# Block maxima of an attention layer: the float16 split moved to GpSimd, the turn moved behind the next burst of scores, the copy moved to ScalarE

## The chip, the cores and the metric

The kernel runs on one core of one Trainium2 chip. The core has five engines that run their own instruction streams and meet at semaphores: TensorE (PE in the profile, with its weight loads listed apart as PEld), VectorE (DVE), ScalarE (ACT), GpSimd (POOL) and SyncE (SP), which here only issues DMAs. Each engine works through its instructions in program order, so an instruction that waits holds up everything behind it on its engine. The metric is the device time of one execution in microseconds, the median of several runs.

## What is computed

```python
x = A_x                                            # 1 x 2048 x 512
xn = _layernorm(x, axis=-1)
# attention, 32 heads of 16
qkv = (xn @ wqkv).reshape(B, S, 3, H, Dh).transpose(2, 0, 3, 1, 4)
scores = einsum("bhqd,bhkd->bhqk", q, k) * Dh ** -0.5
o = einsum("bhqk,bhkd->bhqd", softmax(scores), v)
attention = o.transpose(0, 2, 1, 3).reshape(B, S, D) @ wo
# dense part, 512 -> 1792 -> 512
dense = gelu(xn @ w1 + b1) @ w2 + b2
return x + attention + dense
```

The softmax needs, for each query and head, the largest score over all 2048 keys before the exponentials are taken. How this maximum reaches the exponentials is what the change is about.

## The kernel before

**Blocks and units.** A block `t` is four heads (a group `g`) by 512 queries; there are 8 x 4 = 32 blocks. The attention loop is `unit` (line 766), called once for each of 32 x 16 = 512 units `u`. A unit does one sixteenth of two blocks at once. For block `u // 16` it forms four pieces of scores (`s_half`, one for each head: 128 queries by 512 keys into a PSUM bank of the "S" rotation) and VectorE takes the largest along the keys (`s_max`, line 366) into `mt`. For the block of unit `e = u - 19` (`LEAD` is 19) it forms the transposed scores again (`e_half`, 128 keys by 512 queries into a bank of the "T" rotation), ScalarE takes the exponential (line 414), and TensorE multiplies the exponentials of a unit or two earlier with the values (`v_half`, into `pV`). So a block's maxima are complete three units before its first exponential.

**Two halves of a unit.** TensorE's part of a unit is two halves. Each half begins with a burst of four score pieces (E, S, S, E) and goes on with `v_half` on 64 rows of the array beside the dense work (`dense`: projections, the hidden layer, the second product, the output projection) on the other 64 rows. How many dense products a half takes is the pace: `FAST` four, `SLOW` three, `MEAN` three and four by turns. All products of the loop have line 169 (`tiled`); tiles tell them apart: `pS<-kst,qst`, `pT<-qst,kst`, `pV<-pe,vv`, `pD`.

**The maxima.** The maximum is not subtracted by an instruction of its own: it is written, as two float16 numbers (a high part and the rest), into two spare rows of the stacked queries `qst`, and a constant in the same rows of `kst` makes the product subtract it. The way there, for each block: when the last piece of scores is reduced, `s_end` (line 375) takes the largest of the four partial maxima, negated, into `mneg` (line 382, VectorE). In the next unit, after its first half, `store` (lines 385 to 399) runs: TensorE turns `mneg` with an identity (line 390, float32) into a PSUM bank, VectorE splits the result into the two float16 parts (lines 393 and 394), SyncE stores them to DRAM in two DMAs (line 397) and, once these have landed, loads them into the rows of `qst` in four DMAs, one for each head (`m_rows`, line 348). `e_half` of the block's first unit waits for these loads.

**Which bank.** The turn takes a bank of the S or of the T rotation, three banks each: S where the dense group has just begun (`fresh`, line 387), T otherwise. A bank can be written when its last reader is done: VectorE for S, ScalarE for T.

**GpSimd's work** (splitting weights, GELU, scaling the attention output) is queued as steps; `run_steps` (line 315) lets out up to `POOL_NS` (2500 ns by the kernel's own estimates) for each unit.

**The first block** goes through a planner (`Plan`, line 215) that orders the prologue of the program by estimated times; lines 1130 to 1152 give it the same chain with costs.

Of the kernel before, what the change touches and what calls it, by code (L numbers as in the profile page):

```python
# [18 lines left out]
P = 128  # L19
# [15 lines left out]
POOL_NS = 2500  # L35
TAIL = 5
# [18 lines left out]
def layer_kernel(ctx: ExitStack, tc: tile.TileContext, x, wqkv, wo, w1, b1, w2, b2, out):  # L55
# [19 lines left out]
    m_d = dram.tile([NG * NQB, 16, 2, P], F16, name="m_d")  # L75
# [21 lines left out]
    mnegs = [const.tile([P, 32], F32, name=f"mneg{i}") for i in range(2)]  # L97
    for m in mnegs:
        nc.gpsimd.memset(m, 0.0)
# [244 lines left out]
    def m_rows(t, h):  # L344
# [3 lines left out]
        nc.sync.dma_start(dst, m_d[t, 4 * h:4 * h + 4].rearrange("t r q -> r t q"))  # L348
# [11 lines left out]
    def s_max(u, n, s):  # L360
# [5 lines left out]
        nc.vector.reduce_max(mt_of[t][:, n, qt, kb:kb + 1], s, axis=AX.X)  # L366
# [8 lines left out]
    def s_end(u):  # L375
# [4 lines left out]
        g, qb = divmod(t, NQB)  # L380
        mneg = mnegs[t % 2]
        nc.vector.tensor_reduce(mneg[:, :16], mt_of[t].rearrange("p h t k -> p (h t) k"), axis=AX.X, op=ALU.max, negate=True)
        given("dve", 220)

        def store():

            fresh = cur[0] is not None and 0 < sum(cur[0].at) <= 4
            pt = banks("S" if fresh else "T")
            for a in range(2):
                nc.tensor.matmul(pt[32 * a:32 * a + 32, :64], mneg[64 * a:64 * a + 64, :],  # L390
                                 ident[64 * a:64 * a + 64, 64 * a:64 * a + 64], start=True, stop=True)
            mhl = work.tile([64, 2, 64], F16, name="mhl", bufs=2)
            nc.vector.tensor_scalar_mul(mhl[:, 0], pt[:64, :64], 1.0 / MROW)
            nc.vector.scalar_tensor_tensor(mhl[:, 1], pt[:64, :64], 1.0 / MROW, mhl[:, 0], op0=ALU.mult, op1=ALU.subtract)
            given("dve", 300)
            for a in range(2):
                nc.sync.dma_start(m_d[t, :, :, 64 * a:64 * a + 64], mhl[32 * a:32 * a + 16])
            for h in range(4):
                m_rows(t, h)
# [366 lines left out]
    def unit(gen):  # L766
# [7 lines left out]
        for a in range(2):  # L774
            for kind, b in ((1, 1), (0, 0), (0, 1), (1, 0)) if a == 0 else ((1, 2), (0, 3), (0, 2), (1, 3)):
# [4 lines left out]
                elif not kind and u > NU:  # L780
                    spare(gen, b % 2)
            if e >= 0:
# [23 lines left out]
            if a == 0 and u % 16 == 0 and u // 16 - 1 in stores:  # L806
# [711 lines left out]
```

## Time and profile before

| | |
|---|---|
| median of 3 runs | 1454.23 us (1451.61 to 1455.41) |
| the profiled execution | 1450.86 us, of it the profile's span 1449.1 us |
| mean granted TensorE clock | 0.996 |
| 31 final reductions, line 382 | 220 ns each |
| 31 pairs of split instructions, lines 393 and 394 | 207 and 217 ns each |
| 62 stores, line 397 | 591 ns median issue time each |
| 128 loads, line 348 | 258 ns median issue time each |

The profile lists for each engine how long it was busy, groups of like instructions with their mean duration, who waited for whom, and the instructions in order of time. A row of such a timeline has the start (us from the span's start), the length, the engine, the line, the operation with its output and inputs, a count where like instructions were merged, and in brackets the idle time ahead with what ended it.

### The profile page before, as it was taken

The page shows a single profiled execution, that of the slowest core. Times are in us where ns is not written, and L with a number is a line of the kernel's source. Part 1 is how long each engine was busy: PE and PEld are TensorE (multiplying, and loading weights), DVE is VectorE, ACT ScalarE, POOL GpSimd, SP SyncE. Part 2 cuts the span into 40 slices and gives each one's busy share as a digit, 9 for nine tenths or more (in the row PEclk, how much of TensorE's full clock was granted, in tenths as well). Part 3 has the DMA queues.
Part 4 walks back from the last instruction along what each step waited for, and adds up shares of the span by engine and source line. Part 5 has one row for each costly group of instructions (what it writes and reads, how often), then busy time and mean ns, then how long its engine had stood idle before and what let it go on. Part 6 is the DMA issues. An engine that isn't in the chain of part 4 may idle for free.

```text
span 1449.1 us, 88687 instructions
## 1 busy us (share of the span) xinstructions
PE 1432.0 (99%) x40184; PEld 964.6 (67%) x40184; DVE 1353.8 (93%) x2304; ACT 1255.9 (87%) x2367; POOL 663.8 (46%) x673
## 2 busy tenths in 40 slices
PE   8999999999999999999999999999999999999998
PEld 4447767776666767667677766676766767666565
DVE  7989999999999999999999999999999999999933
ACT  5868888888999888899988899998889999888885
POOL 3201857664878401388831138882115787121100
PEclk9999999999999999999999999999999999999999
DMA  7731565455224210221112111121112110111423
GB/s 218 226 122 40 163 202 182 150 181 153 86 64 131 67 34 27 62 70 42 45 44 89 30 37 46 55 74 45 44 39 85 48 38 23 56 55 47 137 65 119
DMA packets 112627, 124.86 MB, mean 86 GB/s; under 512 B 22908, under 2 KB 84220, under 8 KB 112248
## 3 DMA queue, kind: packets, MB, share of 16 engines
q1 hardware_dynamic: 112248, 119.18, 26.8%
q8 instruction: 314, 5.14, 1.5%
q14 instruction: 65, 0.53, 0.1%
HBM read 81.66 MB, written 37.34 MB: 82 GB/s over the span
## 4 chain that ended last, share of the span: by engine, by line
PE 87%; DVE 8%; DMA 2%; ACT 1%; issue 1%; SPq 0%; DVEq 0%; ACTq 0%
PE pD L169 26%; PE pV L169 25%; PE pT L169 17%; PE pS L169 16%; DVE mt L366 7%; PE pT L1015 2%; DMA wq<-in_A_wqkv_dram 1%; PE pD L1015 1%; DMA m_d<-mhl 0%; ACT xs L968 0%; DVE xt L998 0%; ACT pe L414 0%; DMA qst<-m_d 0%; DVE ac L1393 0%; ACT wqk_h L904 0%
## 5 line engine op out<-in xcount | busy, mean ns | idle before, releaser
L366 DVE TENSOR_REDUCE mt<-pS 128x1 f32<-128x512 f32 x2029 | 1277.4, 682 | 34.8 <-PE pS L169 7.8
L414 ACT ACTIVATE pe<-pT 128x512 f32<-128x512 f32 x2048 | 1106.9, 599 | 150.2 <-PE pT L169 65.0
L169 PE MATMUL pV<-pe,vv 64*32 64x512 f32 x8192 | 1087.8, 591 | 0.3 <-issue 0.2
L169 PE MATMUL pT<-qst,kst 64*32 64x512 f16 x8192 | 710.4, 378 | 1.9 <-issue 1.2
L169 PE MATMUL pS<-kst,qst 62*32 62x512 f16 x8116 | 627.0, 378 | 2.6 <-DVE mt L366 2.0
L169 PEld LDWEIGHTS <-qst 62*32 62x32 f16 x8192 | 309.3, 90 | 196.7 <-issue 50.9
L169 PE MATMUL pD<-xb,wc 64*32 64x512 f16 x5376 | 363.9, 375 | 0.0
L169 PE MATMUL pD<-w_s,g 64*32 64x512 f16 x5376 | 361.8, 375 | 0.0
L169 PEld LDWEIGHTS <-kst 64*32 64x32 f16 x8192 | 280.5, 91 | 96.0 <-issue 24.2
L169 PEld LDWEIGHTS pV<-pe,vv 64*32 64x32 f32 x8192 | 245.3, 105 | 13.6 <-PE pV L169 4.2
L169 PEld LDWEIGHTS <-wc 64*32 64x32 f16 x5376 | 160.7, 91 | 44.5 <-issue 0.4
L169 PEld LDWEIGHTS <-g 64*32 64x32 f16 x5376 | 163.5, 91 | 39.2 <-issue 0.5
L169 PE MATMUL pD<-xt,wqk_h 64*32 64x512 f16 x2400 | 159.3, 376 | 0.7 <-issue 0.7
L1360 POOL TENSOR_TENSOR xa<-xa,yt 128x512 f32<-128x512 f32 x16 | 20.5, 1281 | 222.8 <-ACT yt L1358 222.8
L471 POOL TENSOR_TENSOR osb<-osb,rb 128x512 f32<-128x512 f32 x31 | 39.9, 1286 | 159.2 <-DMA rb<-den_d 132.8
L1312 POOL TENSOR_TENSOR t<-hh 128x512 f32<-128x512 f32 x56 | 58.2, 1040 | 77.0 <-ACT hh L1335 75.9
L169 PEld LDWEIGHTS <-wqk_h 64*32 64x32 f16 x2400 | 74.0, 92 | 19.9 <-issue 2.0
L1314 POOL TENSOR_TENSOR t<-t,hh 128x512 f32<-128x512 f32 x56 | 71.8, 1282 | 4.7
L1307 POOL TENSOR_TENSOR t<-t,hh 128x512 f32<-128x512 f32 x56 | 71.7, 1280 | 4.7
L1309 POOL TENSOR_TENSOR g<-t,g 128x512 f16<-128x512 f32 x56 | 65.2, 1164 | 4.7
L1306 POOL TENSOR_SCALAR t<-t,gs 128x512 f32<-128x512 f32 x56 | 38.8, 694 | 54.8 <-ACT t L1301 54.8
L169 PE MATMUL pD<-wo_s,oc 64*32 64x512 f16 x816 | 54.7, 376 | 0.0
(165 smaller groups left out, 895.1 us busy)
## 6 DMA issues: line engine op xcount, KB each, us to landing
wc<-w_d SPq DMA_DIRECT2D x56, 256.0 KB
qk_d<-stg SPq DMA_DIRECT2D x32, 256.0 KB
rb<-den_d SPq DMA_DIRECT2D x124, 64.0 KB
wch<-in_B_w_dram SPq DMA_DIRECT2D x14, 512.0 KB
wch<-in_B_w_dram SPq DMA_DIRECT2D x28, 256.0 KB
w_d<-wsp SPq DMA_DIRECT2D x28, 256.0 KB
kst<-qk_d SPq DMA_DIRECT2D x64, 96.0 KB
qst<-qk_d SPq DMA_DIRECT2D x64, 96.0 KB
```

The source lines that it names most:

```text
L169: p = nc.tensor.matmul(*args, **kw)
L366: nc.vector.reduce_max(mt_of[t][:, n, qt, kb:kb + 1], s, axis=AX.X)
L414: nc.scalar.activation(pe, st, AF.Exp, scale=scale_of[g // 2])
L471: pooled((1280, lambda: nc.gpsimd.tensor_tensor(osb, osb, rb, op=ALU.mult)), (620, lambda: nc.gpsimd.tensor_scalar(ot[:, 0], osb, 1.0, 0.0 ...
L1015: nc.tensor.matmul(tl[key], lhs, rhs, start=c + n == 0, stop=(c, n) == (NC - 1, 2))
L1306: pooled((690, lambda: nc.gpsimd.tensor_scalar(t1, t1, 1.0, gs[:, 1:2], op0=ALU.add, op1=ALU.mult)), (1280, lambda: nc.gpsimd.tensor_tenso ...
L1307: (1280, lambda: nc.gpsimd.tensor_tensor(t1, t1, hh, op=ALU.mult)),
L1309: (1160, lambda: nc.gpsimd.tensor_tensor(g[:, 1, f, :], t1, g[:, 0, f, :], op=ALU.subtract)),
L1312: pooled((1040, lambda: nc.gpsimd.tensor_tensor(t1, hh, hh, op=ALU.mult)), (620, lambda: nc.gpsimd.tensor_scalar(t1, t1, 1.0, 1.0 / GELU_A ...
L1314: (1280, lambda: nc.gpsimd.tensor_tensor(t1, t1, hh, op=ALU.mult)),
L1360: add = lambda: nc.gpsimd.tensor_tensor(xa, xa, yt, op=ALU.add)
```

## The change

The maxima take another way from `mt` to `qst`. VectorE still takes the largest of the partial maxima (now `mx`, not negated). GpSimd then scales it and makes the two float16 parts, in three instructions on 128 partitions by 16 numbers, put on its queue at the end of the block's last unit, without regard to the allowance of `run_steps`. TensorE turns the float16 parts with a negated float16 identity (`nident`); this now stands behind the burst of the second half of the next unit, ahead of that half's `v_half` and dense work. ScalarE copies the turned parts out of PSUM (64 x 64). One DMA stores them, and two load them (one for each half of the partitions). The allowance of GpSimd's steps becomes 800 ns in the unit before a block's last, and 3100 ns in the three units from the block's last on. The first block's chain in the planner is changed alike. The order of the heads in `mt` is swapped so that a half of the partitions holds its two heads side by side.

```diff
+POOL_AT = {15: 800, 0: 3100, 1: 3100, 2: 3100}
...
-    m_d = dram.tile([NG * NQB, 16, 2, P], F16, name="m_d")
+    m_d = dram.tile([NG * NQB, 2, 2, 2, 8, P // 2], F16, name="m_d")
...
+    nident = const.tile([P, P // 2], F16, name="nident")
+    for a in range(2):
+        nc.gpsimd.tensor_scalar(nident[64 * a:64 * a + 64], ident[64 * a:64 * a + 64, 64 * a:64 * a + 64], -1.0, 0.0,
+                                op0=ALU.mult, op1=ALU.add)
...
     def run_steps(all_of_them=False):
-        room[0] = min(room[0], 0) + POOL_NS
+        room[0] = min(room[0], 0) + (POOL_AT.get(pos[0] % 16, POOL_NS) if pos[0] < NU else POOL_NS)
...
+    def m_store(t, turned):
+        nc.sync.dma_start(m_d[t].rearrange("s a j r q -> (s a j r) q"), turned)
+
+    def m_rows(t, a):
         g, qb = divmod(t, NQB)
-        p, a = divmod(h, 2)
-        dst = qst[g % 2][qb][64 * a + 62:64 * a + 64, p].rearrange("r (t q) -> r t q", q=P)
-        nc.sync.dma_start(dst, m_d[t, 4 * h:4 * h + 4].rearrange("t r q -> r t q"))
+        dst = qst[g % 2][qb][64 * a + 62:64 * a + 64].rearrange("j p (t s q) -> j (p t) s q", s=2, q=P // 2)
+        nc.sync.dma_start(dst, m_d[t, :, a].rearrange("s j r q -> j r s q"))
+
+    def m_parts(t):
+        mx = work.tile([P, 2, 8], F32, name="mx", bufs=1)
+        parts = work.tile([P, 2, 2, 8], F16, name="mparts", bufs=2)
+        return (lambda: nc.vector.tensor_reduce(mx.rearrange("p a r -> p (a r)"), mt_of[t].rearrange("p h t k -> p (h t) k"),
+                                                axis=AX.X, op=ALU.max),
+                lambda: nc.gpsimd.tensor_scalar(mx, mx, 1.0 / MROW, 0.0, op0=ALU.mult, op1=ALU.add),
+                lambda: nc.gpsimd.tensor_scalar(parts[:, :, 0], mx, 1.0, 0.0, op0=ALU.mult, op1=ALU.add),
+                lambda: nc.gpsimd.tensor_tensor(parts[:, :, 1], mx, parts[:, :, 0], op=ALU.subtract)), parts
+
+    def m_turn(pt, parts):
+        for s in range(2):
+            nc.tensor.matmul(pt[32 * s:32 * s + 32, :64], parts[64 * s:64 * s + 64].rearrange("p a j r -> p (a j r)"),
+                             nident[64 * s:64 * s + 64], start=True, stop=True)
+
+    def m_copy(pt):
+        turned = work.tile([64, 64], F16, name="mturned", bufs=2)
+        nc.scalar.activation(turned, pt[:64, :64], AF.Copy)
+        return turned
...
     def s_end(u):
...
-        mneg = mnegs[t % 2]
-        nc.vector.tensor_reduce(mneg[:, :16], mt_of[t].rearrange("p h t k -> p (h t) k"), axis=AX.X, op=ALU.max, negate=True)
+        steps, parts = m_parts(t)
+        for step in steps:
+            step()
...
             pt = banks("S" if fresh else "T")
+            m_turn(pt, parts)
+            m_store(t, m_copy(pt))
             for a in range(2):
-                nc.tensor.matmul(pt[32 * a:32 * a + 32, :64], mneg[64 * a:64 * a + 64, :],
-                                 ident[64 * a:64 * a + 64, 64 * a:64 * a + 64], start=True, stop=True)
-            mhl = work.tile([64, 2, 64], F16, name="mhl", bufs=2)
-            nc.vector.tensor_scalar_mul(mhl[:, 0], pt[:64, :64], 1.0 / MROW)
-            nc.vector.scalar_tensor_tensor(mhl[:, 1], pt[:64, :64], 1.0 / MROW, mhl[:, 0], op0=ALU.mult, op1=ALU.subtract)
-            given("dve", 300)
-            for a in range(2):
-                nc.sync.dma_start(m_d[t, :, :, 64 * a:64 * a + 64], mhl[32 * a:32 * a + 16])
-            for h in range(4):
-                m_rows(t, h)
+                m_rows(t, a)
...
     def unit(gen):
...
+            if a == 1 and u % 16 == 0 and u // 16 - 1 in stores:
+                stores.pop(u // 16 - 1)()
             if e >= 0:
                 one_more()
                 enter()
...
             if a == 0:
                 run_lane()
-            if a == 0 and u % 16 == 0 and u // 16 - 1 in stores:
-                stores.pop(u // 16 - 1)()
```

**TensorE, block 11, first unit of the next block.** Before, the turn (`ident,mneg`) stands between the first half's dense products (`pD`) and the second half's burst (`pT` first; `kst_3_82` and `qst_2_89` are two of the stacked tiles).

```order
L169 LDWEIGHTS g
L169 MATMUL pD<-w_s,g 32x512
L390 MATMUL pT<-ident,mneg_101 32x64 x2
L169 LDWEIGHTS kst_3_82
L169 MATMUL pT<-qst_2_89,kst_3_82 32x512
```

With the change the last rows of that burst come first, then the turn, then the second half's products with the values.

```order
L171 LDWEIGHTS kst_3_82
L171 MATMUL pT<-qst_2_89,kst_3_82 32x512
L366 LDWEIGHTS mparts
L366 MATMUL pT<-nident,mparts 32x64
L366 LDWEIGHTS mparts
L366 MATMUL pT<-nident,mparts 32x64
L171 MATMUL pV<-pe,vv 32x512 x4
L171 LDWEIGHTS g
L171 MATMUL pD<-w_s,g 32x512
```

The turn moved behind one burst of 16 products; nothing else moved between the two places. Apart from these turns TensorE's rows after the prologue are the same in both.

**VectorE, the same block.** Before, two instructions of the split stand behind the first two reductions of the next block's scores.

```order
L458 RECIPROCAL dn<-dn 64x32
L366 TENSOR_REDUCE mt<-pS 128x1 x20
L382 TENSOR_REDUCE mneg_101<-mt 128x16
L366 TENSOR_REDUCE mt<-pS 128x1 x2
L393 TENSOR_SCALAR mhl<-pT 64x64
L394 SCALAR_TENSOR_TENSOR mhl<-pT,mhl 64x64
L366 TENSOR_REDUCE mt<-pS 128x1 x42
```

With the change all 44 reductions up to the next reciprocal follow the final one without a break.

```order
L475 RECIPROCAL dn<-dn 64x32
L390 TENSOR_REDUCE mt<-pS 128x1 x20
L358 TENSOR_REDUCE mx<-mt 128x16
L390 TENSOR_REDUCE mt<-pS 128x1 x44
L475 RECIPROCAL dn<-dn 64x32
```

VectorE lost the two split instructions and kept the rest in place.

**GpSimd at the end of block 8.** These are the rows of the changed kernel: the last step of one piece of GELU, the three new instructions, and the next piece of GELU (`t` and `hh` are its work tiles, `osb` is attention output to be scaled).

```order
L1318 TENSOR_TENSOR g<-t_12839,g 128x512
L360 TENSOR_SCALAR mx<-mx 128x16
L361 TENSOR_SCALAR mparts<-mx 128x2x8
L362 TENSOR_TENSOR mparts<-mx,mparts 128x2x8
L1321 TENSOR_TENSOR t_13494<-hh 128x512
L1322 TENSOR_SCALAR t_13494<-t_13494 128x512
L1323 TENSOR_TENSOR t_13494<-t_13494,hh 128x512
L488 TENSOR_TENSOR osb<-osb,rb 128x512
```

Before, the rows of GELU followed each other directly; the three new ones now stand between them, and the first of the three waits for VectorE's final reduction.

More of the change, by code (lines that the diff above doesn't have):

```diff
@@ L95, in layer_kernel @@
     sexp = const.tile([P, 4], F32, name="sexp")
-    mnegs = [const.tile([P, 32], F32, name=f"mneg{i}") for i in range(2)]
-    for m in mnegs:
-        nc.gpsimd.memset(m, 0.0)
+    nident = const.tile([P, P // 2], F16, name="nident")
+    for a in range(2):
+        nc.gpsimd.tensor_scalar(nident[64 * a:64 * a + 64], ident[64 * a:64 * a + 64, 64 * a:64 * a + 64], -1.0, 0.0,
+                                op0=ALU.mult, op1=ALU.add)
     free_banks = {"S": [0, 1, 2], "T": [3, 4, 5], "D": [6], "V": [7]}
```

31 lines of the change are left out of this document (11 added, 20 removed).

## The prediction

> **What bounds the kernel now.** I read the page first (busy shares), then the waits, then the timelines of VectorE, TensorE and ScalarE around the ends of three blocks.
>
> ```profile
> PE 1432.0 (99%) x40184; PEld 964.6 (67%) x40184; DVE 1353.8 (93%) x2304; ACT 1255.9 (87%) x2367; POOL 663.8 (46%) x673
> ```
>
> TensorE is never long without work, VectorE is close behind. So a gain must come from stretches in which TensorE runs below its pace, which a busy share hides. What the waits name at the maxima is small:
>
> ```profile
> PE pS L169 <- DVE mt L366: 2.0, 5, 1.2
> PEld L169 <- DMA qst<-m_d: 2.8, 5, 0.9
> ```
>
> (columns: us in total, times, longest). The loads of the maxima cost 2.8 us in five places. Pace says more. In block 11, in the stage where the dense work alternates between three and four products, the starts of the value products tell the halves apart:
>
> ```profile
> 548.50 0.66 PE L169 MATMUL pV<-pe,vv 64*32 64x512 f32 x4
> 550.89 0.65 PE L169 MATMUL pV<-pe,vv 64*32 64x512 f32 x4
> 552.34 0.60 PE L169 MATMUL pV<-pe,vv 64*32 64x512 f32 x3
> 553.89 0.61 PE L169 MATMUL pV<-pe,vv 64*32 64x512 f32 x4
> 556.28 0.61 PE L169 MATMUL pV<-pe,vv 64*32 64x512 f32 x4
> 558.89 0.68 PE L169 MATMUL pV<-pe,vv 64*32 64x512 f32 x4
> ```
>
> Units of 2.39 us (548.50 to 550.89, 553.89 to 556.28) alternate with one of 2.61 (556.28 to 558.89). The unit with the turn takes 3.00 (550.89 to 553.89) where 2.62 is due: 0.38 too much. VectorE and TensorE at that place:
>
> ```profile
> 551.24 0.22 DVE L382 TENSOR_REDUCE mneg<-mt 128x16 f32<-128x64 f32 x1
> 551.37 1.28 DVE L366 TENSOR_REDUCE mt<-pS 128x1 f32<-128x512 f32 x2
> 552.57 0.21 DVE L393 TENSOR_SCALAR mhl<-pT 64x64 f16<-64x64 f32 x1
> 552.95 13.23 DVE L366 TENSOR_REDUCE mt<-pS 128x1 f32<-128x512 f32 x21
> 553.67 0.40 PE L169 MATMUL pS<-kst,qst 62*32 62x512 f16 x4
> ```
>
> I call the start of L382 T. The split holds VectorE from 552.57 to 552.95, 0.38 us. The reduction that starts at 552.95 (0.68 us by the mean below) ends at 553.63, and the score piece at 553.67 starts 0.04 later: it waited for that bank.
>
> ```profile
> L366 DVE TENSOR_REDUCE mt<-pS 128x1 f32<-128x512 f32 x2029 | 1277.4, 682 | 34.8 <-PE pS L169 7.8 <-PE pT L169 6.5 <-PE pV L169 2.3
> ```
>
> Where the dense work takes four products in every half, TensorE is slower than VectorE and the loss is smaller. Block 22, by the starts of every second pair of exponentials (so unit by unit), and two more rows of that place:
>
> ```profile
> 1003.57 1.08 ACT L414 ACTIVATE pe<-pT 128x512 f32<-128x512 f32 x2 [0.27 <-PE pT L169]
> 1006.18 1.08 ACT L414 ACTIVATE pe<-pT 128x512 f32<-128x512 f32 x2 [0.27 <-PE pT L169]
> 1008.97 1.09 ACT L414 ACTIVATE pe<-pT 128x512 f32<-128x512 f32 x2 [0.37 <-PE pT L169]
> 1011.59 1.09 ACT L414 ACTIVATE pe<-pT 128x512 f32<-128x512 f32 x2 [0.27 <-PE pT L169]
> 1006.22 0.22 DVE L382 TENSOR_REDUCE mneg<-mt 128x16 f32<-128x64 f32 x1
> 1007.43 0.66 PE L169 MATMUL pV<-pe,vv 64*32 64x512 f32 x4
> ```
>
> 2.61, 2.79, 2.62: 0.18 too much. The third kind is the turn in a bank of S, seven of the 31 blocks behind the first:
>
> ```profile
> L393 DVE TENSOR_SCALAR mhl<-pS 64x64 f16<-64x64 f32 x7 | 1.5, 207 | 0.1
> 922.16 0.61 PE L169 MATMUL pV<-pe,vv 64*32 64x512 f32 x4
> 922.64 1.28 DVE L366 TENSOR_REDUCE mt<-pS 128x1 f32<-128x512 f32 x2
> 923.98 0.40 PE L169 MATMUL pS<-kst,qst 62*32 62x512 f16 x4 [0.20 <-DVE mt L366]
> 924.19 0.61 PE L169 MATMUL pV<-pe,vv 64*32 64x512 f32 x4
> ```
>
> The turn takes one of three banks, so the last score piece of the burst needs the bank of the reductions that end at 923.92 (922.64 + 1.28). This half takes 2.03 us (922.16 to 924.19) against some 1.31 (half of 2.62): 0.7 too much. With 14, 10 and 7 blocks of the three kinds (the 14 and 10 are my sorting of the other 24 by their dense work) the block ends cost 14 x 0.38 + 10 x 0.18 + 7 x 0.7 = 12 us. That bounds the gain from above, with 2.8 for the loads.
>
> **The change part by part. VectorE** loses 0.38 us at each block end, and its reductions come that much earlier. **GpSimd** gets three instructions of 128x16, which the trace doesn't have; the nearest rows are
>
> ```profile
> L472 POOL TENSOR_SCALAR ot<-osb 128x512 f16<-128x512 f32 x31 | 19.1, 618 | 2.7
> L1218 POOL TENSOR_SCALAR wsp<-wch 128x1024 f16<-128x1024 f32 x14 | 14.6, 1045 | 1.1
> L473 POOL TENSOR_TENSOR ot<-osb,ot 128x512 f16<-128x512 f32 x31 | 36.1, 1164 | 2.6
> L1219 POOL TENSOR_TENSOR wsp<-wch,wsp 128x1024 f16<-128x1024 f32 x14 | 30.0, 2141 | 1.2
> ```
>
> One source: 1045 - 618 = 427 ns for 512 numbers more, so 618 - 427 = 191 ns remain for none, and 16 numbers make 204. Two sources: 977 for 512, 187 for none, 218 for 16. Between dependent steps the 31 rows of L473 show 2.6 us of idle time, 0.08 each; I take 0.08 for every hand-over, between engines too (the piece above needed 0.04). From T: 0.22 + 0.08 + 0.20 + 0.08 + 0.20 + 0.08 + 0.22 + 0.08 = 1.16 us until TensorE may load the parts. My bounds are 0.7 (half of 204 for each, and 0.04 a hand-over) and 1.8 (twice 204 each): estimates from these rows in both directions.
>
> The Trainium skill, "GPSIMD Engine Reference", section 4.1, says that elementwise work belongs on VectorE, with GpSimd about twice as slow for two inputs. The trace agrees in kind for wide tiles (L473's 1164 ns against 684 for VectorE's two-source row below); for 16 numbers no row shows it. By that rule the parts would come later than 1.16, which is the second rival.
>
> ```profile
> L998 DVE TENSOR_TENSOR xt<-pT,xt 128x512 f16<-128x512 f32 x6 | 3.9, 684 | 0.0
> ```
>
> **The turn.** When does TensorE come to it? In block 11 the value products that follow it start at T + 1.10 (552.34), in block 22 at T + 1.21 (1007.43). The float32 turn ahead of the burst leaves; in block 22, 0.18 covers it and the reductions, so I give it 0.1. The natural place is T + 1.0 and T + 1.1, the parts are ready at 1.16, and with 0.05 for two small float16 products the values start at T + 1.21: 0.11 later than now in the first kind, unchanged in the second. All that stands behind the turn on TensorE (values, dense work, the next burst) waits with it.
>
> In the first kind the next half then no longer waits for VectorE: the bank that was free at 553.63 is free at 553.25. The values due at T + 1.21 = 552.45 plus 1.31 are at 553.76, against 553.89: 0.13 gained. Second kind: only the rest behind the turn can go, which I put at half of 0.18, 0.09. Third kind: the turn, now behind two S pieces, needs the very bank whose reduction ends at 923.92, so values follow at some 924.05 instead of 924.19: 0.14. Sum: 14 x 0.13 + 10 x 0.09 + 7 x 0.14 = 1.8 + 0.9 + 1.0 = **3.7 us**.
>
> **ScalarE** gets a copy of 64 numbers behind the burst's last exponential. Rows:
>
> ```profile
> L957 ACT ACTIVATE sd<-sd 128x4 f32<-128x4 f32 x4 | 0.8, 209 | 0.7 <-DVE sd L955 0.7
> L509 ACT ACTIVATE ot<-pS 64x512 f16<-64x512 f32 x1 | 0.6, 590 | 2.2 <-DMA out_dram<-ac 2.2
> ```
>
> Between them 64 numbers make 0.25 us (bounds 0.21 and 0.59). ScalarE idles 0.37 ahead of the exponential at 1008.97 in block 22, which covers it; without cover it costs up to 0.25 x 31 = 8 us. I take 0.
>
> **Stores and loads.**
>
> ```profile
> 553.05 1.59 SPq L397 DMA_DIRECT2D m_d<-mhl  x2
> L462 SPq DMA_DIRECT2D den_d<-dn x31: 471/482/1407, 160.4 to 1409.7; - x31
> 763.83 1.15 SPq L348 DMA_DIRECT2D qst<-m_d  x4
> 765.47 0.40 PE L169 MATMUL pT<-qst,kst 64*32 64x512 f16 x4 [0.24 <-DMA qst<-m_d]
> ```
>
> L462 has the new store's shape (64 pieces of 128 bytes), 0.48 us. In block 22 the pair of exponentials ahead of the copy ends at about T + 2.4 (1007.51 by the gap of 0.37 before 1008.97: 1008.60). Copy and hand-over end at T + 2.7, the store's issue at 3.2. In block 11 the two old stores end at 554.64, T + 3.4. So the store is neither earlier nor later by more than some 0.2. Two loads replace four, but the first exponential's row half needs the second issued in both. I take 0 for all of it and leave the 2.8 us of waits where they are. The queue of SyncE gets 1.2 us shorter a block; nothing in the waits shows anyone waiting for that.
>
> **GpSimd's queue.** The three instructions wait for VectorE, and GELU that used to run ahead of T now queues behind them. In block 8:
>
> ```profile
> 426.59 1.29 POOL L1314 TENSOR_TENSOR t<-t,hh 128x512 f32<-128x512 f32 x1
> 437.03 0.63 ACT L1301 ACTIVATE t<-t 128x512 f32<-128x512 f32 x1
> ```
>
> ScalarE takes this result 9.2 us after its end, and behind the new steps (GpSimd is done with them at T + 1.08, T being 428.33 there) and two GELU steps of 1.04 and 0.62 it would end at 432.5 instead of 427.9, 4.6 later. The 9.2 cover it; without cover ScalarE, and soon TensorE, would wait for the remainder. **The prologue** is planned anew in another order: 0, bounds 1 us to either side, as no row tells. **Sum: 3.7 us less**, 1450.86 - 3.7 = 1447.2 on the profiled execution. The median of the runs shown is 3.4 us above that execution, so as a median I expect 1450.5.
>
> **The rivals.** (1) *The parts come in time.* With hand-overs of 0.04 and 0.15 us an instruction they are ready at T + 0.83, ahead of the natural place. Then the first kind saves all but 0.1 of its 0.38, the second 0.12, the third 0.2: 3.9 + 1.2 + 1.4 = 6.5, or 1447.7 as a median (1444.9 if the 2.8 of the loads' waits went as well). For it: the 0.04 above. Against it: the 191 ns that even an empty GpSimd row would take.
>
> (2) *The wait for the parts takes it all* (also the case in which GpSimd is still busy at T, so that the relief is never felt): at 0.27 an instruction the parts come at T + 1.35, values in the first kind at 1.40, and the 0.19 more eat its 0.13 and the 0.09 of the second: 1454 as a median, unchanged. The rule of the Trainium skill on elementwise work ("GPSIMD Engine Reference", section 4.1) leads here.
>
> (3) *Slower: late loads.* The copy is last on ScalarE, behind all exponentials of the burst and any GELU ahead of it. If it ends 0.5 later than I think, the loads do too. Issue to use took 1.64 in block 16 (763.83 to 765.47, which already waits). Of such blocks, about ten of 31 have less than 0.5 to spare, by my reading of where line 348 stands ahead of the use; each loses the full 0.5: 5 us, 3.7 gained, and for 1 us late 18 blocks and 14 us. The price I take is +5 net: 1459. It decides from a copy that ends later than T + 3.0. Against it: the gap of 0.37 on ScalarE.
>
> The Trainium skill, "DMA: Bandwidth & Descriptors", Specifications, asks for transfers of at least 512 bytes, below which the engine reads, modifies and writes. The loads' pieces shrink from 256 to 128 bytes; by that rule they land later, which is rival (3) by another way. The stores of 128 bytes in both kernels show no such step.
>
> **How the numbers follow.** Forecast 0.47, (1) 0.21, (2) 0.22, (3) 0.10. The forecast's own range is 2 to 5.5 us gained, 1448.7 to 1452.2. The range of 1445 to 1455.5 takes in the forecast, (2) with a microsecond and a half for the run, and most of (1); it leaves out (3) and the best end of (1), 0.10 and some 0.05. A measurement tells 0.3%, 4.4 us, from no change. Of the forecast a third lies beyond that (0.16), of (1) nearly all (0.20): faster 0.36. Slower is (3) but for its mild end: 0.09. Same holds the rest, 0.55.
>
> **What would show it.** L393 and L394 are gone and the reductions behind the final one run without a break. The three GpSimd rows: some 0.2 us each, the first 0.3 after T. TensorE's values behind the turn start at about T + 1.2; at 0.9 to 1.1 it is (1), from 1.4 on (2). The unit with the turn in block 11: 2.87 instead of 3.00. In the waits, a new row of TensorE's weight loads for `mparts`; the row for `qst<-m_d` stays near 2.8 us, and well above it (3) holds. What would make all of it wrong: a prologue that moves by several microseconds, or GELU so late behind the new steps that ScalarE waits for it.

## The result, and the profile of the changed kernel

| | before | changed |
|---|---|---|
| median | 1454.23 us (5 runs, 1450.28 to 1455.41) | 1460.82 us (5 runs, 1460.02 to 1461.63) |
| ratio | | 1.0052 (95% interval 1.0035 to 1.0068) |
| the profiled execution, its span | 1450.86, 1449.1 | 1460.86, 1459.0 |

The change makes the kernel 0.5% slower, 7.5 us by the ratio. I had forecast 3.7 us faster. From the page of the changed kernel, the busy times and the chain that ended last, as shares by engine:

```profile
PE 1433.1 (98%) x40120; PEld 946.8 (65%) x40120; DVE 1350.7 (93%) x2240; ACT 1258.2 (86%) x2399; POOL 683.3 (47%) x769
PE 85%; DMA 6%; DVE 5%; ACT 3%; issue 1%; SPq 1%; DVEq 0%; ACTq 0%
```

Busy times say nothing, as before. That DMAs hold 6% of the chain is new: 5% are the store and the loads of the maxima, which held nothing to speak of before, when all DMAs together had 2%. The waits name it (us in total, times, longest):

```profile
PEld L171 <- DMA qst<-m_d: 17.0, 18, 1.5
PE pT L171 <- DMA qst<-m_d: 8.1, 12, 1.0
PEld L366 <- POOL mparts L362: 2.3, 12, 0.4
PE pS L171 <- DVE mt L390: 1.5, 2, 1.2
```

The loads take 17.0 and 8.1, where the same rows of before had 2.8 and 0.6. (All 12 waits of the second row fall on waits of the first, seen by the products instead of the weight loads; the sum, 25.1 us, is a gauge and not a loss of time.) The wait for GpSimd's parts, which I had feared, is 2.3 us. So is the chain up to the store as I drew it? Block 13, in order of time; T is the start of L358:

```profile
642.19 0.22 DVE L358 TENSOR_REDUCE mx<-mt 128x16 f32<-128x64 f32 x1
642.49 0.20 POOL L360 TENSOR_SCALAR mx<-mx 128x16 f32<-128x16 f32 x1 [5.05 <-DVE mx L358]
642.78 0.20 POOL L361 TENSOR_SCALAR mparts<-mx 128x16 f16<-128x16 f32 x1
643.07 0.22 POOL L362 TENSOR_TENSOR mparts<-mx,mparts 128x16 f16<-128x16 f32 x1
643.34 0.20 PE L366 MATMUL pT<-nident,mparts 64*32 64x64 f16 x2
644.07 0.21 ACT L371 ACTIVATE mturned<-pT 64x64 f16<-64x64 f32 x1
644.31 0.47 SPq L347 DMA_DIRECT2D m_d<-mturned  x1
647.76 1.39 SPq L352 DMA_DIRECT2D qst<-m_d  x2
650.47 0.40 PE L171 MATMUL pT<-qst,kst 64*32 64x512 f16 x4 [0.71 <-DMA qst<-m_d]
```

The parts are ready at T + 1.10 and the turn runs at T + 1.15, the copy ends at T + 2.09, the store's issue at T + 2.59. All of that is on time or early. Then two things are slow. The first load waits 2.98 us for the store to land (644.78 to 647.76), and the issues of two loads take 1.39 us, so that the first exponential's product starts at T + 8.28. The issues by line (min/median/max ns), before and after:

```profile
L348 SPq DMA_DIRECT2D qst<-m_d x128: 225/258/298, 90.3 to 1389.6; - x128
```

```profile
L352 SPq DMA_DIRECT2D qst<-m_d x64: 603/658/793, 89.9 to 1399.8; - x64
L347 SPq DMA_DIRECT2D m_d<-mturned x32: 466/476/527, 87.3 to 1396.9; - x32
```

A load costs 658 ns of issue instead of 258. Was the wait for the store's landing there before? SyncE's own waits, before and after:

```profile
SPq L348 <- DMA m_d<-mhl: 51.8, 38, 3.0
```

```profile
SPq L352 <- DMA m_d<-mturned: 54.7, 31, 2.9
```

It was: single waits of 3 us in both. Late stores alone are therefore not new; slow loads are. A second loss lies ahead of the loop: the first exponential's product comes 3.4 us later (before, then after).

```profile
93.18 0.39 PE L169 MATMUL pT<-qst,kst 64*32 64x512 f16 x4
```

```profile
96.60 0.39 PE L171 MATMUL pT<-qst,kst 64*32 64x512 f16 x4
```

### The profile page after: what moved, and what is told of

The parts are those of the page before. It is cut to its first block, busy times and chain, and to the rows that moved or that the text cites. A ratio compares the mean times of both kernels' runs of the same rounds, so it can differ in the third digit from the quotient of the medians.

```text
span 1459.0 us, 88559 instructions
## 1 busy us (share of the span) xinstructions
PE 1433.1 (98%) x40120; PEld 946.8 (65%) x40120; DVE 1350.7 (93%) x2240; ACT 1258.2 (86%) x2399; POOL 683.3 (47%) x769
## 4 chain that ended last, share of the span: by engine, by line
PE 85%; DMA 6%; DVE 5%; ACT 3%; issue 1%; SPq 1%; DVEq 0%; ACTq 0%
PE pD L171 26%; PE pV L171 24%; PE pT L171 18%; PE pS L171 15%; DVE mt L390 3%; DMA m_d<-mturned 3%; DMA qst<-m_d 2%; ACT pe L431 1%; PE pT L1032 1%; SPq L352 1%; DMA qk_d<-stg 0%; DMA wq<-in_A_wqkv_dram 0%; DVE bs L970 0%; DMA kst<-qk_d 0%; DMA xs<-in_A_x_dram 0%
## 5 line engine op out<-in xcount | busy, mean ns | idle before, releaser
L171 PE MATMUL pS<-kst,qst 62*32 62x512 f16 x8116 | 619.2, 378 | 2.0 <-DVE mt L390 1.5
L171 PEld LDWEIGHTS <-qst 62*32 62x32 f16 x8192 | 303.5, 90 | 198.4 <-issue 47.9
L171 PEld LDWEIGHTS pV<-pe,vv 64*32 64x32 f32 x8192 | 239.1, 105 | 14.2 <-PE pV L171 4.6
L360 POOL TENSOR_SCALAR mx<-mx 128x16 f32<-128x16 f32 x32 | 6.5, 204 | 303.9 <-DVE mx L358 293.1
```

Of the source, the lines that this page charges most:

```text
L171: p = nc.tensor.matmul(*args, **kw)
L360: lambda: nc.gpsimd.tensor_scalar(mx, mx, 1.0 / MROW, 0.0, op0=ALU.mult, op1=ALU.add),
```

## The experiments

Twelve runs, of eleven further kernels and of the changed kernel once more, each timed against the kernel before on the same chip (median 1451.5 to 1452.6 us there). "Ratio" is to that kernel, with its 95% interval; differences of ratios are taken of 1452 us.

**Loads in rows of 2048 bytes.** The layout of `m_d` between the store and the loads is turned round, nothing else:

```diff
-    m_d = dram.tile([NG * NQB, 2, 2, 2, 8, P // 2], F16, name="m_d")
+    m_d = dram.tile([NG * NQB, 2, 2, 8, 2, P // 2], F16, name="m_d")
-        nc.sync.dma_start(m_d[t].rearrange("s a j r q -> (s a j r) q"), turned)
+        nc.sync.dma_start(m_d[t].rearrange("a j r s q -> s (a j r) q"), turned)
...
-        nc.sync.dma_start(dst, m_d[t, :, a].rearrange("s j r q -> j r s q"))
+        nc.sync.dma_start(dst, m_d[t, a].rearrange("j r s q -> j (r s q)"))
```

> The changed kernel, with another layout of the DRAM tile between the one store and the two loads: each load now reads and writes two runs of 2048 bytes (one for each of its two partitions) instead of 32 pieces of 128 bytes; the store still writes 64 pieces of 128 bytes. Theory (loads): the changed kernel lost in the issue and landing of its two loads (658 ns of issue each against 258 ns for each of four before, first use 2.9 us after the first issue against 1.64). The issue falls to 0.3 us or less each, the waits of TensorE for qst<-m_d fall from 25.1 to under 6 us in all, and the time falls by the 6.5 us that the loop lost and the 3.7 us that I had forecast to gain, to 1451 (1449 to 1453). Rival (chain): the wait is set by something ahead of the loads (GpSimd, the copy, the store); the waits stay near 25 us and the time stays at 1459 to 1461. Rival (prologue): only the first block's chain lost time, 3.4 us; the waits may fall but the time stays above 1457.

Measured: 1448.5 us, ratio 0.998 (0.997 to 0.9989). No wait for `qst<-m_d` is left among the waits. The issue of the loads, and SyncE's wait for the store:

```profile
L352 SPq DMA_DIRECT2D qst<-m_d x64: 232/242/267, 89.2 to 1386.2; - x64
SPq L352 <- DMA m_d<-mturned: 40.7, 31, 1.5
```

So 1.0052 less 0.998, 10.5 us, was in the loads and the store's landing. It even beats the kernel before. But two things moved: the loads are quick, and the store, now written to two interleaved halves, lands steadily (1.5 us at most). The next runs separate them.

**Four loads, one for each head**, 8 pieces of 256 bytes, as before the change (the parts are laid out head, tile, part, so that the rows fit the old `m_d`):

```diff
...
+        dst = qst[g % 2][qb][64 * a + 62:64 * a + 64, p].rearrange("r (t q) -> r t q", q=P)
+        nc.sync.dma_start(dst, m_d[t, 4 * h:4 * h + 4].rearrange("t r q -> r t q"))
...
```

> The changed kernel with the loads of the kernel before: parts laid out so that the four loads of a block are again one for each head, 8 pieces of 256 bytes each; all ahead of the loads as in the change (GpSimd, the turn, the copy, one store). Theory (loads): issue back to 258 ns each, the waits for qst<-m_d under 6 us, time 1451 (1449 to 1453.5). Rival (chain): the waits stay above 20 us and the time at 1459 to 1461. Rival (prologue): time above 1457 whatever the waits.

Measured: 1450.15 us, ratio 0.9985 (0.9975 to 0.9994), issue 253 ns, no wait for `qst<-m_d` left (its store, too, is interleaved; SyncE's longest wait for it is 1.9 us). The number of loads is not what counts.

**The kernel before with two loads of 128-byte pieces**, its two stores kept but laid out to fit them:

```diff
-            for h in range(4):
-                m_rows(t, h)
+            for a in range(2):
+                m_rows(t, a)
...
-    m_d = dram.tile([NG * NQB, 16, 2, P], F16, name="m_d")
+    m_d = dram.tile([NG * NQB, 16, 2, 2, P // 2], F16, name="m_d")
...
+        nc.sync.dma_start(dst, m_d[t, 8 * a:8 * a + 8].rearrange("r s j q -> j (r s) q"))
```

> The kernel before with nothing changed but the loads: two for each block, each of 32 pieces of 128 bytes, as in the change (the stores keep their two and get no more pieces). Theory (loads): issue some 0.66 us each, the first use some 1.2 us later, waits for qst<-m_d from 3.4 to 20 us or more, and slower than before by some 10 us (1460 to 1467). Rivals (chain, prologue): 1454, unchanged within 2 us.

Measured: 1449.71 us, ratio 0.9987 (0.9978 to 0.9995): no loss at all, my theory of this run fell. (It gains 1.9 us: no wait for `qst<-m_d` is left in it, where the kernel before has five, and its stores, now of 16 runs of 256 bytes, issue in 0.37 us instead of 0.59.) These loads have as many 128-byte pieces as those of the change, and an issue like any other:

```profile
L347 SPq DMA_DIRECT2D qst<-m_d x64: 241/258/293, 90.9 to 1387.6; - x64
```

So neither two loads nor small pieces make the issue slow. The rule of the Trainium skill that I weighed ("DMA: Bandwidth & Descriptors", Specifications, transfers of at least 512 bytes) does not name the cause.

**The first block's chain as before**, all else as in the change (lines 1147 to 1161 of the changed kernel replaced by the old ones, with a DRAM tile of its own; the tile of the turned parts goes from two buffers to one with it):

> The changed kernel with the first block's chain in the prologue as before (VectorE splits, float32 turn, two stores, four loads), so that the planner orders TensorE's prologue as before; all other blocks as in the change. Theory (loads) with the prologue as a second loss of 3.4 us: the first exponential's product comes at 93.2 us instead of 96.6, and the time is 1457.4 (1456.5 to 1458.5); the waits for qst<-m_d stay near 25 us. Rival (the shift of the prologue is regained later or differs from run to run): 1460 to 1461. Rival (prologue alone): 1454.

Measured: 1457.43 us, ratio 1.0044 (1.0031 to 1.0056); first exponential's product at 94.41; waits for `qst<-m_d` 17.1 us. By the ratio that is the rival, whose 1460 to 1461 us are 1.0040 to 1.0047 of 1454.23; the 1457.4 of the theory came out as a time only because the kernel before is faster on this chip. The start did move to the old place, and the waits are lower than the forecast 25 us; 11 of the 31 stores land late in this trace, by the measure given below, against 14. The same edit is tried again below.

**Loads of one dimension less.** I took the slow issue for one of four dimensions in the addresses. Three kernels test that. The first leaves the layout and the store as changed and cuts each load in two:

```diff
-        nc.sync.dma_start(dst, m_d[t, :, a].rearrange("s j r q -> j r s q"))
+        for s in range(2):
+            nc.sync.dma_start(dst[:, :, s], m_d[t, s, a])
```

> The changed kernel with its layout and its one store untouched; each of its two loads is cut in two, by halves of the queries, so that a load has 16 pieces of 128 bytes and one dimension less in its addresses (partition, head and query tile, query). What is left as it was: the store, whose landing the traces show late in about half of the blocks (SyncE waited for it 54.7 us in all, at most 2.9, against 40.7 and 1.5 in the run with rows of 2048 bytes). Theory (the slow part is the issue of a load with four dimensions; the late stores alone are covered): four issues of some 0.25 us each, TensorE's waits for qst<-m_d fall from 25.1 to under 8 us, SyncE's wait for the store stays above 50 us, and the ratio to the kernel before is 0.998 to 1.000 (1448.5 to 1451.5 here). Rival (the late stores are the loss): waits above 15 us and a ratio of 1.003 or more. Rival (pieces of 128 bytes are the loss): issue above 0.5 us each, time as the changed kernel or worse.

Measured: 1501.52 us, ratio 1.0333 (1.0317 to 1.0348). The theory fell. The signs of both rivals came true, so this run does not part them; the kernel before with two loads had ruled out the size of the pieces, and late stores alone are tried below. How far the time moved is telling:

```profile
L353 SPq DMA_DIRECT2D qst<-m_d x128: 574/600/780, 88.8 to 1443.4; - x128
PEld L171 <- DMA qst<-m_d: 58.9, 31, 3.1
PE pT L171 <- DMA qst<-m_d: 43.1, 31, 2.6
```

Half the pieces, and each issue as slow. All four together take 2.64 us from start to end (median of the blocks), 1.26 more than the two of the change (1.38). 31 blocks x 1.26 = 39 us; by the ratios this run is 41 us slower than the changed kernel. Here TensorE waits for the loads in every block (31 waits), and the longer issue comes through nearly whole.

The other two take the layout of the first run with gaps, so that the store is the interleaved one that lands steadily. A row of 128 queries gets five or four places of 64, and its halves stand in places 0 and 2, for the store too:

```diff
+    m_d = dram.tile([NG * NQB, 2, 2, 8, 5, P // 2], F16, name="m_d")
...
+        nc.sync.dma_start(dst, m_d[t, a, :, :, 0:4:2])
```

> The changed kernel with another DRAM layout: rows of 64 numbers, two in every five used, so that a load still has four dimensions in its addresses (partition, head and query tile, half of the queries, query; 32 pieces of 128 bytes) but all near each other, while the store is of the form that landed steadily in the run with rows of 2048 bytes. Theory (four dimensions make the issue slow; the loss needs slow loads and late stores together): issue 0.6 us or more each, SyncE's wait for the store near 41 us with at most 1.5 each, TensorE's waits for qst<-m_d under 10 us, ratio to before 0.998 to 1.001. Rival (slow loads alone are the loss): waits above 15 us, ratio 1.003 or more. Rival (far strides, not dimensions, made the issue slow): issue 0.3 us or less.

> The changed kernel with another DRAM layout: every second row of 64 numbers is left empty, so that a load has 32 pieces of 128 bytes as in the change, but three dimensions in its addresses; the store is of the form that landed steadily. Theory (dimensions): issue 0.3 us or less each, first use as with rows of 2048 bytes, ratio to before 0.9975 to 0.999. Rival (pieces of 128 bytes): issue 0.6 us, landing some 0.3 us later, ratio above 1.000.

Measured: 1450.87 us, ratio 0.999 (0.998 to 0.9999) with five places; 1449.4 us, 0.9984 (0.9976 to 0.9993) with four. The issues, in this order, and what TensorE's weight loads waited in all (us, times):

```profile
L352 SPq DMA_DIRECT2D qst<-m_d x64: 589/616/702, 89.3 to 1386.5; - x64
  PEld L171: 4.3, 14
```

```profile
L352 SPq DMA_DIRECT2D qst<-m_d x64: 605/620/685, 89.8 to 1388.2; - x64
  PEld L171: 3.6, 11
```

Three dimensions are as slow as four, so that part of the theory fell as well. The other part held: slow loads behind a steady store cost almost nothing. What sorts the issues is in the addresses of the program as built, here as steps on the DRAM side and on the side of `qst`:

```
load                        DRAM side           qst side            issue, ns
before, four loads          2 x 4, runs of 128  2 x 4, runs of 128  258, 253
rows of 2048 bytes          2, runs of 1024     2, runs of 1024     242
before with two loads       2 x 16, runs of 64  2 x 16, runs of 64  258
changed                     16 x 2, runs of 64  2 x 16, runs of 64  658
five places                 16 x 2, runs of 64  2 x 16, runs of 64  616
four places                 32, runs of 64      2 x 16, runs of 64  620
changed, loads cut          16, runs of 64      2 x 8, runs of 64   600
```

Every load of the table whose two sides take the same steps issues in 0.24 to 0.26 us, every other in 0.60 to 0.66. Its packets start later, too: in block 16 they begin 0.86 us after the issue's start with two equal sides, 1.44 with unequal ones of the same count and size, and the medians of 31 blocks are 0.86 and 1.45. Equal steps are not the whole of it: the stores take 0.57 to 0.59 us with unequal sides and 0.33 or 0.37 with equal ones of 32 or 16 rows, but the store of the change, 64 rows on both sides, takes 0.48. In the programs as built, the quick loads and those two quick stores carry a mark (`ant_dge_precooked`) that all the others lack; no run parts the mark from the equal steps for a load.

**Late stores with quick loads.** The first run again, with the store cut in two by halves of the queries:

```diff
-        nc.sync.dma_start(m_d[t].rearrange("a j r s q -> s (a j r) q"), turned)
+        for s in range(2):
+            nc.sync.dma_start(m_d[t].rearrange("a j r s q -> s (a j r) q")[s], turned[32 * s:32 * s + 32])
```

> The changed kernel with rows of 2048 bytes for its loads, as in the first run, and with its one store cut in two by halves of the queries, 32 pieces of 128 bytes each. In the traces a store of that shape spreads over 16 DMA engines and lands late when one of them is fetching program code; the single store of the first run used two engines and landed 1.3 to 1.6 us after its issue every time. So this is the fourth cell: late stores with fast loads. Theory (the loss needs late stores and slow loads together): SyncE's wait for the stores has single waits above 2 us again, TensorE's waits for qst<-m_d stay under 8 us, ratio to before 0.998 to 1.000. Rival (late stores alone are enough): waits above 15 us, ratio 1.003 or more.

Measured: 1450.8 us, ratio 0.9994 (0.9981 to 1.0006), waits for `qst<-m_d` 5.3 us, SyncE's wait for the stores 46.7 us with 2.9 at most; the stores of 13 of 31 blocks land more than 2.3 us after the first one's issue began. That is the fourth cell:

| ratio to before | quick loads (0.24 us) | slow loads (0.6 us or more) |
|---|---|---|
| steady store | 0.998 | 0.9984, 0.999 |
| late stores | 0.9994 | 1.0052, and 1.0064 again |

Either alone costs 0.15% or less, hardly more than the intervals; together they cost 0.7 to 0.8%.

**The changed kernel once more:**

> The changed kernel itself once more, on the chip of these runs, for a second trace. Theory: ratio 1.004 to 1.0065 again, TensorE's waits for qst<-m_d 17 to 27 us, stores that land more than 2 us after their issue in 10 to 17 of 31 blocks (which blocks these are may differ), and in those blocks alone a late first exponential. Rival (the profiled run was an odd one): ratio below 1.002.

Measured: 1461.08 us, ratio 1.0064 (1.0048 to 1.008), waits for `qst<-m_d` 25.0 us. Block 13, which was late in the first trace, is on time in this one:

```profile
638.08 0.22 DVE L358 TENSOR_REDUCE mx<-mt 128x16 f32<-128x64 f32 x1
640.21 0.47 SPq L347 DMA_DIRECT2D m_d<-mturned  x1
641.89 1.38 SPq L352 DMA_DIRECT2D qst<-m_d  x2
645.45 0.59 PE L171 MATMUL pT<-qst,kst 64*32 64x512 f16 x7
```

The first load starts 1.21 us behind the store's issue instead of 2.98, and the product comes at T + 7.37 instead of T + 8.28, the time it has with rows of 2048 bytes. The packets of the two stores, in us from the start of the store's issue:

```
block 13                                  first trace       second trace
60 of the store's 64 packets, starts      1.13 to 1.31      1.13 to 1.31
the other four, starts                    2.39 to 2.46      with the others
packet of program code, 16 KB             1.17 to 2.41      1.56 to 2.71
last landing of the store                 3.44              1.67
```

The page lists that traffic as a queue of its own (packets, MB, share):

```profile
q8 instruction: 313, 5.13, 1.5%
```

Over all blocks behind the first: 14 stores of the first trace and 11 of the second landed more than 2.3 us after their issue began. In each of these 25 exactly four of the 64 packets were late, and the first of them started within 0.1 us of the end of a 16-KB packet of code. Against the run with rows of 2048 bytes, the first exponential's product came later by 0.89 us on average (12.5 in all) behind the 14, by 0.05 behind the other 17; in the second trace by 0.95 behind the 11 and 0.10 behind the other 20. So most of the loss sits in the blocks with a late store. The store of the change lands in 16 steps of its semaphore, one for a DMA engine as I read it, and is done with the last of them; the interleaved one lands in two, and SyncE's longest wait for it was 1.5 us. The trace does not name a packet's engine: that the four late packets, a sixteenth of the store, stood behind the fetch of code on one engine is inferred from their number and from these times.

**The turn at its old place**, with rows of 2048 bytes (the call of `stores.pop` goes back behind the first half's dense work):

> The changed kernel with rows of 2048 bytes for its loads, and the turn back at its place before the change, behind the first half's dense work and ahead of the second burst. The parts are ready at T + 1.15 there too, T being the start of the final reduction. Theory: TensorE now stands before the turn with the burst queued behind it and waits some 0.5 to 0.8 us for the parts in each of 31 blocks; its waits for mparts rise from 2.1 to 15 to 25 us, and the ratio to before is 1.006 to 1.014. Rival (the place is indifferent, VectorE is late anyway): ratio 0.998 to 1.000.

Measured: 1457.27 us, ratio 1.0037 (1.0023 to 1.0051).

```profile
PEld L366 <- POOL mparts L362: 27.5, 32, 1.1
PE pT L366 <- POOL mparts L362: 7.4, 22, 0.5
PE pS L366 <- POOL mparts L362: 2.2, 6, 0.5
```

TensorE waits for GpSimd in every block, 0.86 us on average at its weight loads, and loses 8.3 us to the first run. The direction was right. The waits are longer than I had expected (27.5 us for 15 to 25) and the loss is smaller: 0.27 of the 0.86 us a block reach the end.

**The parts by VectorE**, with rows of 2048 bytes:

```diff
+        eng = nc.vector if t else nc.gpsimd
-                lambda: nc.gpsimd.tensor_scalar(mx, mx, 1.0 / MROW, 0.0, op0=ALU.mult, op1=ALU.add),
+                lambda: eng.tensor_scalar(mx, mx, 1.0 / MROW, 0.0, op0=ALU.mult, op1=ALU.add),
...
```

> The changed kernel with rows of 2048 bytes for its loads, and the three instructions that make the parts on VectorE instead of GpSimd, directly behind the final reduction (31 blocks; the first block stays with GpSimd). Theory (what the change gains is VectorE's 0.38 us at each block end): VectorE gives three instructions of 0.1 to 0.2 us each, its reductions come 0.4 us later, the parts some 0.3 us earlier; the gain goes but for what the turn's place brings, ratio to before 1.000 to 1.002. Rival (the gain comes from the turn's place and the shorter stores and loads, not from VectorE): ratio 0.998, as with GpSimd.

Measured: 1486.04 us, ratio 1.0227 (1.0208 to 1.0246). Against the first run (0.998) that is six times the loss I had expected or more.

```profile
L361 DVE TENSOR_SCALAR mx<-mx x31: 174/175/1253, 133.3 to 1420.9; 128x16 f32<-128x16 f32 x31
L362 DVE TENSOR_SCALAR mparts<-mx x31: 174/175/1196, 133.5 to 1421.1; 128x16 f16<-128x16 f32 x31
PE pS L171 <- DVE mt L391: 33.3, 32, 2.2
```

The median is 0.175 us, shorter than GpSimd's 0.204; but some take over a microsecond. The three groups sum to 36.8 us, and the run is 36 us slower than the first (1.0227 less 0.998). TensorE's wait for VectorE's reductions, the last row, had 1.5 us in the first run. Block 19, VectorE and GpSimd:

```profile
905.32 0.82 DVE L361 TENSOR_SCALAR mx<-mx 128x16 f32<-128x16 f32 x1
906.18 0.17 DVE L362 TENSOR_SCALAR mparts<-mx 128x16 f16<-128x16 f32 x1
906.39 0.47 DVE L363 TENSOR_TENSOR mparts<-mx,mparts 128x16 f16<-128x16 f32 x1
```

```profile
904.82 1.29 POOL L489 TENSOR_TENSOR osb<-osb,rb 128x512 f32<-128x512 f32 x1
906.20 0.63 POOL L490 TENSOR_SCALAR ot<-osb 128x512 f16<-128x512 f32 x1
```

The long ones end when GpSimd's instruction ends (906.14 and 906.11; 906.86 and 906.83). Of the 93, 32 took over 0.25 us; all of these started while an instruction of GpSimd ran and ended 0.02 to 0.03 us behind it. Of the 61 short ones three started so, with at most 0.12 us of GpSimd's instruction left. The Trainium skill, "SBUF — State Buffer", section "SBUF: two separate sides", names it: VectorE and GpSimd share a pair of ports, and an instruction that takes the pair (on VectorE only some do) holds it for its whole length. The old split, which read PSUM, had 207 and 217 ns a row. So this run prices the clash with GpSimd, and not what VectorE's relief is worth.

**Rows of 2048 bytes and the first block's chain as before**, the two edits together:

> The changed kernel with rows of 2048 bytes for its loads and with the first block's chain in the prologue as before, so that TensorE's order in the prologue is that of the kernel before. Theory (prologue is a second, smaller loss, some 1.5 to 3 us): the first exponential's product at 93 to 94.5 us instead of 95.9, ratio to before 0.9955 to 0.997 (1445 to 1447). Rival (the start of the loop moves from run to run and the order of the prologue costs nothing): ratio 0.998, as with the rows alone.

Measured: 1447.05 us, ratio 0.9968 (0.9956 to 0.998), the fastest of all. The first exponential's product:

```profile
94.46 0.39 PE L174 MATMUL pT<-qst,kst 64*32 64x512 f16 x4
```

The intervals of this run and of the rows alone overlap, as do those of the other pair (1.0044 and 1.0052). But the start of the loop sorts: 93.2 to 94.5 us in the four traces with the old order, 95.5 or later in all ten with the new one. I take the prologue for a loss of about 0.12%, 1.7 us (the other pair gives 1.2).

## Why the prediction was wrong

The step that failed is the one on **stores and loads**: "Two loads replace four, but the first exponential's row half needs the second issued in both. I take 0 for all of it and leave the 2.8 us of waits where they are." Two of the new loads take 1.38 us to issue where the first two of the old ones took 0.55. I had priced them like the old ones without saying so: the 1.2 us by which SyncE's queue was to get shorter come out only with 0.26 us for each. No row of before had a load whose two sides take different steps, and this cost, unlike GpSimd's and the copy's, got no bounds. Two rows lay near: L462 (0.48 us at 64 pieces), and the old stores, whose sides do differ, with 0.59; two of these are 0.96 and 1.18. The 2.8 us of waits I read as a small cost; they were the sign that the loads had next to no slack in the blocks with a late store, and SyncE's single waits of up to 3.0 us for the old stores could be seen in the trace of before. 0.8 us more of issue and some 0.3 more until the data had landed, felt mostly behind the 14 late stores, gave the 17.0 us of waits at the weight loads and cost 10.5 us.

- **Rival (3)** had the right sign and nearly the right time (1459), by the wrong road, which is luck. It asked for a copy that ends after T + 3.0; behind the first block one of 31 did (T + 3.55), the others ended at T + 2.07 to 2.77. "Against it: the gap of 0.37 on ScalarE" was no argument against slow issues. I gave it 0.10.
- **GpSimd** came as worked out: 204, 203 and 218 ns at the median, parts at T + 1.09 to 1.11 in all blocks (forecast 1.16). Rival (2) is out: the wait for the parts is 2.3 us. The rule of the Trainium skill beside it ("GPSIMD Engine Reference", section 4.1) does not carry over to tiles as small as this: VectorE's median is shorter, 0.175 us, but by far less than half, and with its waits for GpSimd the three instructions cost more there.
- **The values behind the turn**, T + 1.21 forecast, started at T + 1.16 in block 11 (T is 560.48 there). The unit with the turn, 2.87 forecast, took 2.91 (3.00 before):

```profile
560.07 0.65 PE L171 MATMUL pV<-pe,vv 64*32 64x512 f32 x4
561.64 0.64 PE L171 MATMUL pV<-pe,vv 64*32 64x512 f32 x4
562.98 0.59 PE L171 MATMUL pV<-pe,vv 64*32 64x512 f32 x2
```

- **The 3.7 us** of the ends of the blocks: with the loads out of the way (rows of 2048 bytes), the last four units of 30 blocks, by the starts of their first exponentials' products, are 3.3 us shorter than before. 1.8 of that are three blocks (12, 16 and 29) whose loads had been late before, which I had left where they were. 15 of the other 27 gain 0.10 to 0.15 each, which is the size forecast for the first two kinds; the rest gain nothing in sum. The third kind, forecast at 0.14, got -0.09 to 0.10: in block 20 the half with the turn went from 2.03 to 1.88 us, and the one behind it from 1.32 to 1.41. So the mechanism is there, at 1.5 us instead of 3.7. The loop of that trace is 6.1 us shorter in all, from the first exponential's product to that of the last unit; where the 2.8 us outside the block ends come from is open.
- **The copy** at 0.21 us stands in no wait (in block 13 ScalarE idles 0.44 us behind it), and behind the prologue no wait names GpSimd but that of the turn.
- **The prologue**, "0, bounds 1 us to either side", cost some 1.7. TensorE has done 21 products less by 60 us, 335 instead of 356 (first stretch of the windows, before and after: length, then busy us and count of PE, PEld, DVE, ACT and POOL, then clock, DMA share, GB/s):

```profile
0.00:60.00 60.00, 53.05 (x356) 25.11 (x357) 49.05 (x124) 42.13 (x77) 20.71 (x36) 0.94 0.67 208
```

```profile
0.00:60.00 60.00, 50.66 (x335) 24.55 (x336) 50.30 (x122) 40.63 (x74) 20.27 (x36) 0.94 0.67 207
```

Its busy time is 2.4 us less there already, of the 3.4 us by which the first exponential's product comes later. The count sorts all 14 traces, 353 to 356 with the old order and 334 to 341 with the new one. Which step of the new order makes TensorE wait is open.

In sum, by the ratios: the new chain with loads of equal sides, a steady store and the old prologue gives -4.6 us (interval -6.4 to -2.9); the new prologue takes back 1.7; slow loads behind late stores take 10.5. That -4.6 lies near the forecast's -3.7 is luck: in the first run's trace the forecast mechanism shows 1.5 us, 1.8 come from waits for loads that I had not counted on, and the rest is open. The new allowance of GpSimd's steps was not tried alone.

## What to carry to other kernels

Price a DMA by how its addresses run on both sides, and not by its bytes or its count alone: lay the rows in DRAM so that both sides of the load take the same steps, and let the store do the scattering. Small waits behind a chain of DMAs are a gauge of slack: look in every block at how much the chain's longest link varies before adding to it. A small transfer on which something waits was safer on two DMA engines than on 16 here, since it is done when the last one is.

## What the runs showed of the hardware that was not expected

- The issue of a load: 0.24 to 0.26 us with equal steps on both sides, for 2, 8 and 32 pieces alike; 0.60 to 0.66 with unequal ones, for 16 and 32.
- A packet of 16 KB of program code takes 0.9 to 1.5 us (19 of 20 in the changed kernel's trace; the longest 1.9), and a store spread over 16 engines that meets one lands 2.4 to 3.5 us after its issue began instead of 1.7. The Trainium skill, "Runtime: NRT & Kernel Launch", section "Instruction fetch mechanics", has the blocks of 16 KiB and calls the cost of crossing one mostly hidden. That is said of the engine that runs the code; the store that met the fetch paid for it here.
- How many engines a DMA takes follows the rule of the Trainium skill, "DMA: Bandwidth & Descriptors", section "Why a DMA increments its semaphore by 16 and not by 1" (the largest number up to 16 that divides the slowest dimension of both sides): the store of 64 rows landed in 16 steps, its interleaved form, 2 x 32 on the DRAM side, in two.
- VectorE's instruction on 128x16 numbers in SBUF took up to 1.25 us where its median is 0.175: all 32 long ones of 93 ended 0.02 to 0.03 us behind an instruction of GpSimd.
